# The output projection of four tiles in seven half-size products

## The chip, the cores and the metric

The kernel runs on one core of one Trainium2 chip. A core has a matrix engine (TensorE; PE in the profile, with PEld for its weight loads), VectorE (DVE), ScalarE (ACT), GpSimd (POOL) and SyncE (SP). Each takes its own instructions in order. PE writes its results into PSUM, eight banks of 128 partitions by 512 float32 columns; the other engines read operands from SBUF or PSUM, POOL from SBUF only. Semaphores hold an instruction back until the data that it needs are there. The metric is the device time of the program in microseconds, so lower is better.

## The reference

Four sequences of 768 tokens with eight heads of 64 pass through a block-wise linear attention with decay, and its output, 3072 rows of 512, goes through a gated feed-forward block:

```python
for b in range(nb):
    intra = np.einsum('bhic,bhjc->bhij', qb, kb) * Dmask[None]
    intra = np.einsum('bhij,bhjd->bhid', intra, vb)
    inter = np.einsum('bhid,bhde->bhie', qb * lam_pow[None], kv_state)
    out[:, :, sl] = intra + inter
    kv_state = lam_block[None, :, None, None] * kv_state + np.einsum('bhsd,bhse->bhde', kb_dec, vb)
...
g = x @ w_gate
silu = g * (1.0 / (1.0 + np.exp(-g)))
val = x @ w_val
return (silu * val @ w_out).astype(np.float32)
```

`w_gate` and `w_val` are 512 by 1536 and `w_out` is 1536 by 512. The change concerns only the last product, `h @ w_out`, with h = silu * val.

## The kernel before, in words

Tokens are worked off in six tiles (t = 0 to 5) of 512 tokens: four blocks of 128, which come from two attention groups of two blocks each. Group g belongs to tile g // 2.

For one tile the feed-forward part runs over twelve chunks of 128 columns of the hidden width (`ffn_fc`). A chunk is one step of the plan: four matmuls of 512 columns into a bank for the gate (L519), a Silu on ACT into a `sil` tile (L523), four matmuls into the next bank for the value (L534), and a product on DVE that reads that bank and writes one chunk of h in bfloat16 (L537). h is held in two tiles of six chunks each. The output projection `ffn_out` (L544 to L557) makes one block of 128 rows: twelve matmuls with a chunk of h as weights and 512 columns of `wo_sb` as the moving operand, all summed in one bank (L552), then a copy to an `osb` tile (L554) and a store to DRAM (L555). The very last block is made in a part of 384 columns and one of 128, so that its two copies and stores go through different engines.

PSUM banks are handed out in a ring of eight by `bank()`. Whoever takes a bank waits for the last reader of its former contents.

The order of work is written out by hand. `steps` holds the chunks of all tiles, and `plan` says what follows which step: `at(n, fn, ...)` appends a call. In tile t - 1, `attend(2t)` and `attend(2t + 1)` make the attention output that tile t reads. One call of `attend(g)` issues the inter-block matmuls of group g (L466), those for the state update of group g + 1 (L387), the scores of group g + 1 (L357), then the intra-block matmuls of g (L479). It needs v_s of group g + 1 (scaled by POOL, L243), its transposed q and k (`qkt`), and the running state (POOL, L426 to L437). `qkt` comes from `cast_scaled`: ACT casts k (L263), DVE scales q (L265), and SP issues a transposing DMA (L256). The loads of k, q and v go through SP (L107) into `raw` tiles, ten slots, and `v` tiles.

From tile 3 on, `cast_scaled` follows chunks 0 and 6, `attend` follows chunks 4 and 10, and the four output blocks of the tile before follow chunks 0, 3, 7 and 9. In tile 2 they follow chunks 1, 5, 7 and 9. The four blocks of tile 5 come at the end.

```python
for n, o in zip((1, 5, 7, 9) if t == 2 else (0, 3, 7, 9), outs):
    at(sn[n], ffn_out, *o)
outs = [(t, b) for b in range(4)]
```

Of the kernel before, what the change touches and what calls it, by code (L numbers as in the profile page):

```python
# [11 lines left out]
ALU = mybir.AluOpType  # L12
# [25 lines left out]
def _body(ctx, tc, nc, q, k, v, lam, moe_w_gate, moe_w_val, moe_w_out, out):  # L38
# [332 lines left out]
    def upd_mm(g, up=None):  # L371
        b, i = groups[g]
        v_s = st[("vs", g)]
        up = up or [bank() for _ in range(2)]
        started = set()
        for s in range(2):
            for hp in range(HP):
                for r in range(2):
                    if g >= NAT0 and i == NG // B - 1 and 2 * s + r == 3:
                        continue  # L380
                    for h2 in range(2):
                        ps = slice(r * M, r * M + M)
# [130 lines left out]
    def ffn_gate(t, fc, b0=0, b1=B):  # L513
        xt = st[("xt", t)]
        N = (b1 - b0) * BLK
        fs = slice(fc * 128, fc * 128 + 128)
        gp = bank()
        for mc in range(MC):
# [4 lines left out]
        nc.scalar.activation(sil[:, 0:N], gp[:, 0:N], AF.Silu)  # L523

    def ffn_val(t, fc, b0=0, b1=B):
        hn = ("h", t, fc // FH)
        if hn not in st:
            st[hn] = h_pool.tile([128, FH, B, BLK], BF16, name="h", tag="h")
        h_sb, xt, sil = st[hn], st[("xt", t)], st[("sil", t, fc, b0)]
        N = (b1 - b0) * BLK  # L530
        fs = slice(fc * 128, fc * 128 + 128)
        vp = bank()
        for mc in range(MC):
            nc.tensor.matmul(vp[:, 0:N], wv_sb[:, mc, fs],  # L534
                             xt[:, b0 // 2:b1 // 2, mc].rearrange("p g b n -> p g (b n)"),
                             start=(mc == 0), stop=(mc == MC - 1))
        nc.vector.tensor_tensor(out=h_sb[:, fc % FH, b0:b1].rearrange("p b n -> p (b n)"),  # L537
                                in0=sil[:, 0:N], in1=vp[:, 0:N], op=ALU.mult)
# [5 lines left out]
    def ffn_out(t, b, last=False):  # L544
# [3 lines left out]
            if last else ((0, DM, nc.scalar.copy, nc.scalar),)  # L548
        for c0, c1, fn, eng in halves:
            ps = bank()[:, 0:c1 - c0]  # L550
            for fc in range(FC):
                nc.tensor.matmul(ps, st[("h", t, fc // FH)][:, fc % FH, b], wo_sb[:, fc, c0:c1],  # L552
                                 start=(fc == 0), stop=(fc == FC - 1))
# [232 lines left out]
    at(s2, ffn_out, 0, 2)  # L786
    at(s2, ffn_out, 0, 3)

    outs = [(1, b) for b in range(4)]
    for t in range(2, NG // 2):  # L790
        sn = [step(t, fc, 2 if t == 2 and fc < NH else 0) for fc in range(FC)]
        if t == 2:
            at(sn[4], ahead, 6)
            at(sn[5], v_scale, 7, nc.vector)
# [7 lines left out]
        if t + 1 < NG // 2:  # L802
            at(sn[7 if t == 2 else 4], attend, 2 * t + 2)
            at(sn[10], attend, 2 * t + 3)
        for n, o in zip((1, 5, 7, 9) if t == 2 else (0, 3, 7, 9), outs):
            at(sn[n], ffn_out, *o)
        outs = [(t, b) for b in range(4)]

    for n, (t, fc, b0, b1) in enumerate(steps):
        if t >= 1 and t + 1 < NG // 2 and ("xt", t + 1) not in st:  # L810
            new_xt(t + 1)
        ffn_fc(t, fc, b0, b1)
        run_later(pace.get(n, 2 if len(later) > 1 else 1))
        for fn, a in plan.get(n, []):
            fn(*a)
            if fn in (attend, ahead):
                run_later(1)
    run_later(len(later))
    for t, b in outs:
        ffn_out(t, b, last=(b == 3))  # L820
# [1 line left out]
_INS = ['q', 'k', 'v', 'lam', 'moe_w_gate', 'moe_w_val', 'moe_w_out']  # L822
_OUTS = [((3072, 512), 'float32')]
# [25 lines left out]
```

## Time and profile before

| What | Value |
|---|---|
| median of three runs | 227.19 us |
| lowest and highest run | 226.88 and 227.25 us |
| span of the profiled execution, first to last instruction | 225.0 us (the only time given for that execution) |
| granted TensorE clock, mean | 1.000 |
| PE busy | 219.2 us, 97% of the span |
| DVE, ACT, POOL busy | 92.4, 106.5, 88.0 us |
| L519 and L534, gate and value matmuls | 77.2 and 77.1 us, 28% of the chain each |
| L552, output projection matmuls | 65.5 us, 28% of the chain |
| stores of 256 KB from `osb` | 23, median 2.9 us from issue to landing |

Matmuls are pipelined: one of 512 columns is recorded with 379 ns and one of 256 with 273, while they follow each other more closely than that. So the spacing is read from the chain, which shows runs of matmuls with their start and length, and not from the mean of one.

A row of a group gives line, engine, operation, output <- inputs, shapes and count, then busy time and mean of one, then the idle time of the engine just before these instructions and who ended it. In a time line each row is a start, a length, and what ran; the bracket at its end is idle time before it and its releaser. L12 is line 12 of the kernel.

### The profile page before, as it was taken

The numbers are of one execution on the slowest core, as the hardware profiler recorded it, in microseconds if no ns is written. First come the engines' busy times: TensorE is split into PE (matmuls) and PEld (weight loads), VectorE is DVE, ScalarE is ACT, GpSimd is POOL, SyncE is SP. The second block draws the span as 40 slices with busy tenths as digits, with TensorE's granted clock in tenths as the row PEclk, the third lists the DMA queues.
The fourth block names the chain that finished last, engine by engine and source line by source line (L and its number), as shares of the span: only waits on it lengthen the run. The fifth ranks groups of instructions, "written<-read, shape, count | busy, mean of one in ns | idle before, by whom it ended". The sixth has DMA issues, their size and how long they took to land.

```text
span 225.0 us, 6040 instructions
## 1 busy us (share of the span) xinstructions
PE 219.2 (97%) x2504; PEld 122.6 (54%) x2504; DVE 92.4 (41%) x159; ACT 106.5 (47%) x211; POOL 88.0 (39%) x131
## 2 busy tenths in 40 slices
PE   8989999999999999999999999999999999999994
PEld 4666455888886456454544544544544444444442
DVE  2664357576853712835345262253242123222200
ACT  5878586756462433564543543543533423322321
POOL 6674737837691120879553191191150000000000
PEclk9999999999999999999999999999999999999999
DMA  6999999999996999595788939806101101101122
GB/s 195 346 339 343 371 362 321 258 287 206 401 244 142 269 219 204 143 228 149 199 197 209 222 69 246 222 4 139 50 1 47 50 0 47 47 3 47 47 93 93
DMA packets 88028, 39.70 MB, mean 176 GB/s; under 512 B 57666, under 2 KB 83522, under 8 KB 88002
## 3 DMA queue, kind: packets, MB, share of 16 engines
q1 hardware_dynamic: 83490, 32.58, 57.1%
q10 hardware_dynamic: 4512, 6.75, 8.3%
q8 instruction: 19, 0.31, 0.6%
q14 instruction: 7, 0.06, 0.1%
HBM read 28.31 MB, written 6.29 MB: 154 GB/s over the span
## 4 chain that ended last, share of the span: by engine, by line
PE 95%; ACT 2%; DVE 1%; issue 1%; DVEq 0%
PE bank L519 28%; PE bank L534 28%; PE bank L552 28%; PE bank L479 2%; PE bank L466 2%; PE bank L387 2%; PE bank L131 1%; PE bank L331 1%; PE bank L357 1%; PE bank L294 1%; DVE ssb L338 1%; ACT qkt L296 1%; PE bank L166 0%; ACT qdec L188 0%; ACT L639 0%
## 5 line engine op out<-in xcount | busy, mean ns | idle before, releaser
L537 DVE TENSOR_TENSOR h<-sil,bank 128x512 bf16<-128x512 bf16 (+1 forms) x91 | 51.7, 575 | 101.5 <-PE bank L534 82.2
L519 PE MATMUL bank<-xt,wg_sb 128*128 128x512 bf16 (+1 forms) x364 | 77.2, 335 | 0.0
L534 PE MATMUL bank<-xt,wv_sb 128*128 128x512 bf16 (+1 forms) x364 | 77.1, 335 | 0.0
L523 ACT ACTIVATE sil<-bank 128x512 bf16<-128x512 f32 (+1 forms) x91 | 46.2, 512 | 42.9 <-PE bank L519 37.9
L552 PE MATMUL bank<-wo_sb,h 128*128 128x512 bf16 (+2 forms) x300 | 65.5, 371 | 0.0
L534 PEld LDWEIGHTS <-wv_sb 128*128 128x128 bf16 x364 | 35.4, 98 | 27.1 <-DVE wv_sb L689 0.5
L519 PEld LDWEIGHTS <-wg_sb 128*128 128x128 bf16 x364 | 34.4, 98 | 26.0 <-DVE xt L491 0.2
L552 PEld LDWEIGHTS <-h 128*128 128x128 bf16 x300 | 28.7, 98 | 32.6
L554 ACT COPY osb<-bank 128x512 f32<-128x512 f32 (+1 forms) x24 | 14.0, 582 | 56.2 <-PE bank L552 56.2
L243 POOL TENSOR_TENSOR v_s<-v,dec 128x1024 bf16<-128x1024 f32 (+1 forms) x14 | 21.7, 1556 | 20.7 <-DMA v<-in_v_dram 17.8
L426 POOL TENSOR_TENSOR kvf<-kvs,ups 128x256 f32<-128x256 f32 x8 | 5.8, 727 | 40.3 <-ACT ups L409 37.8
L338 DVE TENSOR_TENSOR ssb<-bank,causal 128x512 bf16<-128x512 f32 x24 | 15.4, 684 | 4.9 <-PE bank L331 4.9
L435 POOL CAST kvn<-kvf 64x256 bf16<-64x256 f32 x24 | 12.5, 520 | 1.5
L491 ACT CAST xt<-bank 128x512 bf16<-128x512 f32 x19 | 11.6, 658 | 3.0 <-PE bank L479 2.0
L426 POOL TENSOR_TENSOR kvf<-kvf,ups 128x256 f32<-128x256 f32 x16 | 11.6, 726 | 0.6
L409 ACT COPY ups<-bank 128x256 f32<-128x256 f32 (+1 forms) x24 | 9.5, 450 | 1.4 <-PE bank L387 0.9
L263 ACT CAST qk<-kraw 128x1024 bf16<-128x1024 f32 x9 | 9.4, 1043 | 0.8 <-DMA kraw<-in_k_dram 0.8
L265 DVE TENSOR_TENSOR qk<-qraw,qdn 128x1024 bf16<-128x1024 f32 x6 | 8.0, 1328 | 2.1 <-DMA qraw<-in_q_dram 2.1
L362 DVE TENSOR_TENSOR ssb<-bank,causaln 128x512 bf16<-128x512 f32 x12 | 8.3, 688 | 1.2 <-PE bank L357 1.1
L479 PE MATMUL bank<-ssb,v_s 64*64 64x128 bf16 (+1 forms) x384 | 6.7, 207 | 0.3 <-ACT guard L450 0.3
L387 PE MATMUL bank<-v_s,qk 64*64 64x64 bf16 x352 | 5.8, 195 | 0.5 <-issue 0.5
L479 PEld LDWEIGHTS <-v_s 64*64 64x64 bf16 x384 | 5.5, 105 | 1.3 <-issue 0.7
(68 smaller groups left out, 124.9 us busy)
## 6 DMA issues: line engine op xcount, KB each, us to landing
out_dram<-osb ACTq DMA_DIRECT2D x23, 256.0 KB, 2.9
v<-in_v_dram SPq DMA_DIRECT2D x18, 256.0 KB, 4.6
woraw<-in_moe_w_out_dram SPq DMA_DIRECT2D x6, 512.0 KB, 7.7
kraw<-in_k_dram SPq DMA_DIRECT2D x24, 128.0 KB, 3.6
qraw<-in_q_dram SPq DMA_DIRECT2D x24, 128.0 KB, 3.6
wraw<-in_moe_w_gate_dram SPq DMA_DIRECT2D x5, 512.0 KB, 6.9
wraw<-in_moe_w_val_dram SPq DMA_DIRECT2D x5, 512.0 KB, 6.9
kraw<-in_k_dram SPq DMA_DIRECT2D x4, 512.0 KB, 6.6
```

Source lines behind the costliest of these rows:

```text
L243: eng.tensor_tensor(out=st[("vs", g)][:, h0:h1], in0=st[("v", g)][:, h0:h1].rearrange("p h (s d) -> p h s d", s=2), in1=vfac(g, h0, h1), o ...
L338: nc.vector.tensor_tensor(out=ssb[:, h2, 2 * c:2 * c + 2].rearrange("p a s n -> p a (s n)"), in0=sp[(c, h2)].rearrange("p (a x) -> p a x", ...
L426: nc.gpsimd.tensor_tensor(out=o, in0=f, in1=u, op=ALU.add)
L435: nc.gpsimd.tensor_copy(out=o[64 - h2 * 64:128 - h2 * 64], in_=f[h2 * 64:h2 * 64 + 64])
L479: nc.tensor.matmul(op[r][h2 * 64:h2 * 64 + 64, cols(g, hp, s)], v_s[ps, 2 * hp + h2, s], ssb[ps, h2, hp * 2 + s] if g >= NAT0 else ssb[ps, ...
L491: fns[r](out=xt[:, g % 2, :, r].rearrange("p h (m s) -> p h s m", s=2) if g < NAT0 else xt[:, g % 2, :, :, r * M:r * M + M], in_=op[r].rea ...
L519: nc.tensor.matmul(gp[:, 0:N], wg_sb[:, mc, fs], xt[:, b0 // 2:b1 // 2, mc].rearrange("p g b n -> p g (b n)"), start=(mc == 0), stop=(mc = ...
L523: nc.scalar.activation(sil[:, 0:N], gp[:, 0:N], AF.Silu)
L534: nc.tensor.matmul(vp[:, 0:N], wv_sb[:, mc, fs], xt[:, b0 // 2:b1 // 2, mc].rearrange("p g b n -> p g (b n)"), start=(mc == 0), stop=(mc = ...
L537: nc.vector.tensor_tensor(out=h_sb[:, fc % FH, b0:b1].rearrange("p b n -> p (b n)"), in0=sil[:, 0:N], in1=vp[:, 0:N], op=ALU.mult)
L552: nc.tensor.matmul(ps, st[("h", t, fc // FH)][:, fc % FH, b], wo_sb[:, fc, c0:c1], start=(fc == 0), stop=(fc == FC - 1))
L554: fn(out=osb[:, c0:c1], in_=ps)
```

## The change

The projection of tiles 2 to 5 goes from `ffn_out` to `out_units`. A unit is one group: its two blocks of 128 rows are the two row blocks of a 2 by 2 scheme. The inner dimension is split into chunks 0 to 5 and 6 to 11 of h, and the output columns into two halves of 256. Strassen's scheme in Winograd's form makes the four quarter results from seven products of a quarter's size, each six matmuls of 256 columns, where eight products would be made directly.

The products need sums of operands. On W: three tiles `wt` and one that replaces the upper right quarter of `wo_sb`, each made in three pieces (`wo_combo`). On h: for a pair of chunks (two from each half), four instructions (`h_combo`); three results go to new tiles `hs`, and one replaces the odd blocks of the first half of h. All are DVE instructions on bfloat16 in SBUF. `wt` and `hs` take slots of the `raw` pool.

A unit uses three banks. The first product goes into bank `a`; ACT copies it into bank `b`, where later products add to it without clearing it. [...] The second product goes into bank `e`, and ACT copies it to an SBUF tile `es`. DVE twice adds `b` and `es`: once into bank `e`, once into the output tile. ACT copies the other three quarters, and each unit makes two stores of 256 KB.

The order changes too. In tiles 3 to 5 the chunks run in the order 0, 1, 6, 7, 2, 3, 8, 9, 4, 5, 10, 11, so that a pair is complete after every four steps. The two units of a tile follow steps 5 and 8 of the next tile. The operand sums follow single steps, one to three at a time; the last pair of a tile is summed after steps 0 to 3 of the next. In the tables of steps below `sn[n]` is the n-th step of tile t. The last tile's two units come at the end, their first two products one unit after the other, then the other five of each.

```diff
+    def take(n, seeded, cols):
+        was = [primed.get((ring[0] + i) % 8, 0) >= cols for i in range(n)]
+        got = [bank() for _ in range(n)]
+        j = was.index(True)
+        got[seeded], got[j] = got[j], got[seeded]
+        return got
...
+    def wo_combo(n, j):
+        fs, fz = slice(2 * j, 2 * j + 2), slice(FH + 2 * j, FH + 2 * j + 2)
+        b11, b12 = wo_sb[:, fs, 0:HD], wo_sb[:, fs, HD:DM]
+        b21, b22 = wo_sb[:, fz, 0:HD], wo_sb[:, fz, HD:DM]
+        if n < 3 and n not in wt:
+            wt[n] = raw_pool.tile([128, FH, HD], BF16, name="wt", tag="raw")
+        w = [wt[i][:, fs] if i in wt else None for i in range(3)]
+        o, i0, i1 = ((w[0], b12, b11), (w[1], b22, w[0]), (w[2], b21, w[1]), (b12, b22, b12))[n]
+        nc.vector.tensor_tensor(out=o, in0=i0, in1=i1, op=ALU.subtract)
+
+    def h_combo(t, j, n, eng=nc.vector):
+        fs = slice(2 * j, 2 * j + 2)
+        ha, hb = st[("h", t, 0)], st[("h", t, 1)]
+        a11, a21 = ha[:, fs, 0:B:2], ha[:, fs, 1:B:2]
+        a12, a22 = hb[:, fs, 0:B:2], hb[:, fs, 1:B:2]
...
+        s = [st[("hs", t, i)][:, fs] for i in range(3)]
+        o, i0, i1, op = ((s[0], a21, a22, ALU.add), (s[1], s[0], a11, ALU.subtract),
+                         (a21, a11, a21, ALU.subtract), (s[2], a12, s[1], ALU.subtract))[n]
+        eng.tensor_tensor(out=o, in0=i0, in1=i1, op=op)
...
+    def out_units(t, gs):
...
+        for g in gs:
+            bs = take(3, 1, HD)
+            u[g] = ([x[:, 0:HD] for x in bs],
+                    [osb_pool.tile([128, DM], FP32, name="osb", tag="osb") for _ in range(2)],
+                    kv_pool.tile([128, HP, D], FP32, name="es", tag="kvf", bufs=4).rearrange("p h d -> p (h d)"))
+
+        def product(g, k, lhs, rhs, start):
+            o = u[g][0][k]
+            for fc in range(FH):
+                nc.tensor.matmul(o, lhs(fc), rhs(fc), start=(start and fc == 0), stop=(fc == FH - 1),
+                                 skip_group_check=True)
...
+        for g in gs:
+            (a, b, e), (o0, o1), es = u[g]
+            product(g, 0, lambda f: ha[:, f, 2 * g], lambda f: wo_sb[:, f, 0:HD], True)
+            nc.scalar.copy(out=b, in_=a)
+            product(g, 2, lambda f: ha[:, f, 2 * g + 1], lambda f: wo_sb[:, f, HD:DM], True)
+            nc.scalar.copy(out=es, in_=e)
+        for g in gs:
+            (a, b, e), (o0, o1), es = u[g]
+            product(g, 1, lambda f: s2[:, f, g], lambda f: wt[1][:, f], False)
+            nc.vector.tensor_tensor(out=e, in0=b, in1=es, op=ALU.add)
+            product(g, 0, lambda f: hb[:, f, 2 * g], lambda f: wo_sb[:, FH + f, 0:HD], False)
+            nc.scalar.copy(out=o0[:, 0:HD], in_=a)
+            product(g, 1, lambda f: s1[:, f, g], lambda f: wt[0][:, f], False)
+            nc.vector.tensor_tensor(out=o1[:, HD:DM], in0=b, in1=es, op=ALU.add)
+            product(g, 2, lambda f: hb[:, f, 2 * g + 1], lambda f: wt[2][:, f], False)
+            nc.scalar.copy(out=o1[:, 0:HD], in_=e)
+            store(g, 1)
+            product(g, 1, lambda f: s4[:, f, g], lambda f: wo_sb[:, FH + f, HD:DM], False)
+            nc.scalar.copy(out=o0[:, HD:DM], in_=b)
+            store(g, 0)
...
-    outs = [(1, b) for b in range(4)]
+    outs = [(ffn_out, 1, b) for b in range(4)]
...
-        sn = [step(t, fc, 2 if t == 2 and fc < NH else 0) for fc in range(FC)]
+        order = [c for j in range(FC // 4) for c in (2 * j, 2 * j + 1, FH + 2 * j, FH + 2 * j + 1)]
+        sn = [step(t, fc, 2 if t == 2 and fc < NH else 0) for fc in (range(FC) if t == 2 else order)]
...
-        for n, o in zip((1, 5, 7, 9) if t == 2 else (0, 3, 7, 9), outs):
-            at(sn[n], ffn_out, *o)
-        outs = [(t, b) for b in range(4)]
+        for n, o in zip((1, 5, 7, 9) if t == 2 else (5, 8), outs):
+            at(sn[n], *o)
+        if t == 2:
+            for n in range(9):
+                at(sn[n + 2], wo_combo, n // 3, n % 3)
+            for n in range(4):
+                at(sn[8 + n], h_combo, t, 0, n)
+        else:
+            for n in range(4):
+                at(sn[4 + n], h_combo, t, 0, n)
+                at(sn[8 + n], h_combo, t, 1, n)
+                if t == 3:
+                    at(sn[n // 2], h_combo, t - 1, 1, n)
+                    at(sn[2 + n // 2], h_combo, t - 1, 2, n)
+                else:
+                    at(sn[n], h_combo, t - 1, 2, n)
+                if t == 3 and n < 3:
+                    at(sn[n], wo_combo, 3, n)
+        outs = [(out_units, t, (g,)) for g in range(2)]
...
-    for t, b in outs:
-        ffn_out(t, b, last=(b == 3))
+    for n in range(4):
+        h_combo(NG // 2 - 1, 2, n)
+    out_units(NG // 2 - 1, (0, 1))
```

More of the change, by code (lines that the diff above doesn't have):

```diff
@@ L78, in _body, with covered @@
     ring = [0]
+    primed = {}
     def bank():
         b = banks[ring[0] % 8]
+        primed[ring[0] % 8] = 0
         ring[0] += 1
         return b
+    def covered(cols, n=1):
+        for i in range(n):
+            primed[(ring[0] - 1 - i) % 8] = cols
     def gsrc(t, g, h0):
@@ L373, in upd_mm @@
         v_s = st[("vs", g)]
-        up = up or [bank() for _ in range(2)]
+        if up is None:
+            up = [bank() for _ in range(2)]
+            covered(HP * D, 2)
         started = set()
@@ L496, in core_a @@
         st[("op", g)] = [bank() for _ in range(2)]
+        covered(2 * HP * D, 2)
         inter(g, True)
@@ L517, in ffn_gate @@
         gp = bank()
+        covered(N)
         for mc in range(MC):
@@ L532, in ffn_val @@
         vp = bank()
+        covered(N)
         for mc in range(MC):
@@ L550, in ffn_out @@
             ps = bank()[:, 0:c1 - c0]
+            covered(c1 - c0)
             for fc in range(FC):
@@ L557, in ffn_out @@
                           in_=osb[:, c0:c1])
+    def take(n, seeded, cols):
[4 more added lines that the diff above has]
+        return got
+    HD = DM // 2
+    wt = {}
+    def wo_combo(n, j):
[7 more added lines that the diff above has]
+        nc.vector.tensor_tensor(out=o, in0=i0, in1=i1, op=ALU.subtract)
@@ new lines, in h_combo @@
+    def h_combo(t, j, n, eng=nc.vector):
[3 more added lines that the diff above has]
+        a12, a22 = hb[:, fs, 0:B:2], hb[:, fs, 1:B:2]
+        for i in range(3):
+            if ("hs", t, i) not in st:
+                st[("hs", t, i)] = raw_pool.tile([128, FH, B // 2, BLK], BF16, name="hs", tag="raw")
+        s = [st[("hs", t, i)][:, fs] for i in range(3)]
+        o, i0, i1, op = ((s[0], a21, a22, ALU.add), (s[1], s[0], a11, ALU.subtract),
+                         (a21, a11, a21, ALU.subtract), (s[2], a12, s[1], ALU.subtract))[n]
+        eng.tensor_tensor(out=o, in0=i0, in1=i1, op=op)
@@ new lines, in out_row, with store @@
+    def out_row(t, b):
+        g = groups[2 * t + b // 2]
+        return g[0] * S + (g[1] * 2 + b % 2) * BLK
+    def out_units(t, gs):
+        ha, hb = st[("h", t, 0)], st[("h", t, 1)]
+        s1, s2, s4 = [st[("hs", t, i)] for i in range(3)]
+        u = {}
+        for g in gs:
[8 more added lines that the diff above has]
+                                 skip_group_check=True)
+        def store(g, r):
+            nc.scalar.dma_start(out=bass.AP(tensor=out.tensor, offset=out.offset + out_row(t, 2 * g + r) * DM,
+                                            ap=[[DM, 128], [1, DM]]), in_=u[g][1][r])
+        for g in gs:
[18 more added lines that the diff above has]
+            store(g, 0)
@@ L787, in _body @@
     at(s2, ffn_out, 0, 3)
-    outs = [(1, b) for b in range(4)]
+    outs = [(ffn_out, 1, b) for b in range(4)]
+    late_steps = {}
     for t in range(2, NG // 2):
-        sn = [step(t, fc, 2 if t == 2 and fc < NH else 0) for fc in range(FC)]
+        order = [c for j in range(FC // 4) for c in (2 * j, 2 * j + 1, FH + 2 * j, FH + 2 * j + 1)]
+        sn = [step(t, fc, 2 if t == 2 and fc < NH else 0) for fc in (range(FC) if t == 2 else order)]
         if t == 2:
@@ L813, in _body @@
         run_later(pace.get(n, 2 if len(later) > 1 else 1))
-        for fn, a in plan.get(n, []):
+        for fn, *a in [(f, *x) for f, x in plan.get(n, [])]:
             fn(*a)
```

## The prediction

> **What bounds the kernel now.** I read the page first (who is busy, the chain), then the chain in order of time, then the groups with their shapes kept apart, then the time lines of DVE, POOL and SP around tiles 2 and 3.
>
> ```profile
> PE 219.2 (97%) x2504; PEld 122.6 (54%) x2504; DVE 92.4 (41%) x159; ACT 106.5 (47%) x211; POOL 88.0 (39%) x131
> ...
> PE 95%; ACT 2%; DVE 1%; issue 1%; DVEq 0%
> ```
>
> PE is busy 97% of the span and makes 95% of the chain: time goes only if PE's list shortens, and any wait that PE newly meets is paid in full.
>
> ```profile
> 69.07 0.44 PE bank L534 x4
> 69.51 2.59 PE bank L552 x12
> ...
> 114.80 2.59 PE bank L552 x12
> ...
> 126.89 0.38 PE bank L466 x32
> ...
> 211.49 10.40 PE bank L552 x60
> ```
>
> These are pieces of the chain (start, length, matmuls). Four 256-column matmuls take 0.44 us; eleven such pieces, 64.70 to 69.51, make 4.81/44 = 0.1093 us each. Twelve of 512 columns take 2.59, 0.216 each. The 2.59 at 114.80 is the output block at tile 3's chunk 0; 126.89 is the attention of group 8 (chunk 4). The last tile's projection, 10.40, ends at 221.89, the span 3.1 later.
>
> ```profile
> L537 DVE TENSOR_TENSOR h<-sil,bank 128x512 bf16<-128x512 bf16 x53 | 36.4, 688 | 83.2 <-PE bank L534 77.1 <-ACT sil L523 4.5 <-PE bank L331 1.5
> ...
> L537 DVE TENSOR_TENSOR h<-sil,bank 128x256 bf16<-128x256 bf16 x38 | 15.3, 418 | 18.3 <-ACT sil L523 13.1 <-PE bank L534 5.2
> ...
> L300 DVE TENSOR_TENSOR qkt<-bank,qdec 128x256 bf16<-128x256 bf16 x12 | 2.8, 284 | 0.2 <-PE bank L294 0.2
> ```
>
> The price of one two-operand DVE instruction. With a float32 bank, 256 more columns cost 270 ns (418 to 688), so 148 ns are fixed. L300, all of 16 bits (its bank holds bfloat16), takes 284 for 256 columns, 136 above the fixed part: half the rate.
>
> ```profile
> 114.91 0.69 DVE L537 TENSOR_TENSOR h<-sil,bank 128x512 bf16<-128x512 bf16 x1
> 117.67 1.23 DVE L265 TENSOR_TENSOR qk<-qraw,qdn 128x1024 bf16<-128x1024 f32 x1 [2.07 <-DMA qraw<-in_q_dram]
> 119.22 0.69 DVE L537 TENSOR_TENSOR h<-sil,bank 128x512 bf16<-128x512 bf16 x1 [0.33 <-PE bank L534]
> ```
>
> ```profile
> 119.53 1.91 POOL L243 TENSOR_TENSOR v_s<-v,dec 128x1024 bf16<-128x1024 f32 x1 [3.71 <-DMA v<-in_v_dram]
> ...
> 131.97 1.90 POOL L435 CAST kvn<-kvf 64x256 bf16<-64x256 f32 x2
> ```
>
> ```profile
> 119.04 1.91 SPq L256 DMA_TRANSPOSE qkt<-qk  x1
> ```
>
> At tile 3's chunk 0 DVE stands 2.07 us for group 9's q, then scales it (L265), and only then may multiply chunk 1. That costs nothing now, for the output block keeps PE busy from 114.80 to 117.39. The pair of POOL casts took 1.90 us, against 0.85 for the pair at 129.10: L265 ran from 132.40 to 133.62 and the second cast ended just after it.
>
> **The change part by part.**
>
> *Products.* Before, a unit (two blocks) is 24 matmuls of 0.216 = 5.18 us. After, it is 7 x 6 = 42 of 0.1093 = 4.59. Eight units save 8 x 0.59 = 4.7 us. Their weight loads (98 ns each in the rows) go beside the stream: the 0.1093 was taken where every matmul loads its own.
>
> [...]
>
> *Handovers inside a unit.* Consumers start 0.04 (ACT) or 0.11 us (DVE) after a piece ends (136.00 to 136.04; 131.68 to 131.79), and PE resumes 0.2 after them: 0.04 (178.09 to 178.13) and the 0.16 by which a 256-column matmul's 273 ns outlast its spacing. A product lasts 0.656. The seed copy takes the 0.381 of L409's 256-column row: 0.04 + 0.38 + 0.2 = 0.62, hidden by the next product. Each of the two DVE additions over `b` takes the 0.418 of L537: 0.11 + 0.42 + 0.2 = 0.73, hidden but for 0.075. So 0.15 a unit, 1.2 in all. No row has an engine write a float32 sum into a bank: from 0 (284 ns, the cheapest row) to 0.7 a unit (688 ns). I take 418, the same columns with one bank operand. If ACT's Silu or DVE's h product stood in front, up to 0.6 would come on top; at chunks 5 and 8 both are done by then.
>
> *Operand sums.* 12 on W and 12 a tile on h, of 512 bfloat16 columns: 60 DVE instructions. By L300's rate 148 + 272 = 0.42 us, 0.40 from start to start (neighbours overlap by up to 0.08). Bounds: 0.28 (L300 as it is) and 0.69 (L537). L300 is nearest, its operands being all of 16 bits. That is 24 us on an engine 59% idle: free except in two places.
>
> *First place: tile 3, chunks 0 to 4.* Tile 2 runs on PE as before, so chunk 0 still ends at 114.80. The output blocks of chunks 0 and 3 are gone (units now follow chunks 5 and 8), so PE reaches chunk 4's end at 114.80 + 4 x 1.727 = 121.71 and group 9's scores, after 0.38 + 0.25 of attention matmuls, at 122.34. DVE is held by q until 117.67 as now; SP's loads are not moved. Behind the scaling come 3 sums, h of chunk 1, 3 sums, h of chunk 2, 3 sums, h of chunk 3: 118.80 + 9 x 0.40 + 2 x 0.61 + 0.69 = 124.3. The scores take the two banks of chunk 3 (eight banks in a ring: chunk 3, chunk 4, two, two, then these), so they wait for that h: 124.5 instead of 122.34, 2.2 us. In this stretch POOL's v_s of group 9 (1.91, ready at 119.53) meets the sums. It can start at the latest beside h of chunk 1, about 120.0, and keeps the next sums from 120.6 to 121.9; DVE lost 0.38 of 0.52 us of overlap at 90.82 (1.60 instead of 1.22), about 0.7 of it, so 0.9 more: **3.1 us**; without the clash 2.2, and the time 228.4. The floor is SP's transpose, issued at 119.04, landing 3.9 later, 122.9: 0.8. The ceiling is with sums at 0.61 apart: 5.0.
>
> That POOL's cast waited out all of L265 is the row for this. [...] No run here shows it for 16-bit sums.
>
> *Other attention steps.* In tile 2, 9 W sums and 4 h sums can hold POOL back by 0.42 each; before group 6's attention (98.02) POOL ends its state at 96.88 and three sums lie in between, 1.26: 0.1. Group 10 comes after 10.4 us of PE instead of 15.6; its chain (scaling, transpose 3.7 to 5.0 to land) just fits: 0.2, at most 0.8. SP's q of group 11 may wait for a `raw` slot until chunk 8's unit; v queues behind it; both land some 2 us before use: 0.
>
> *Second place: the end.* After chunk 11, DVE has h (0.11 to 0.80), one sum left of pair 1, then three until a11-a21 of pair 2: four at about 0.42 from 0.72, so 2.4, and PE goes on at 2.6. PE has product `a` and four of six matmuls of `e` before it, 1.09. So 1.5 us (1.0 to 2.5). Before, eleven matmuls of the first block covered it.
>
> Two units at once want four `osb` out of three: the fourth waits for the first store to land. A late store takes 2.0, which just reaches: 0.2 (0 to 0.6).
>
> The last store is 256 KB behind a 0.38 copy: 0.07 + 0.38 + 0.02 + 2.0 + 1.1 (from the 64 KB's landing, 222.29 + 1.6, to 225.0) = 3.6 against 3.1: 0.5.
>
> **Sum.** -4.7 + 1.2 + 3.1 + 0.1 + 0.2 + 1.5 + 0.2 + 0.5 = +2.1 us. The only time shown for an execution with a profile is its span, 225.0; the runs have 227.19, 2.2 more for what lies around it, which I keep. 225.0 + 2.1 = 227.1; **229.3 us.**
>
> **Rivals.**
> 1. *DVE keeps up* (ends on the other side). If the sums come every 0.24 us or less, h of chunk 3 is ready when the transpose lands, and the first place costs 0.8: 227.0. If the seams are then hidden too (-1.2), 225.8. For: L300 at 284 has fewer columns only. Against: it would need 512 columns at less than L300 takes for 256. That point, h of chunk 3 by 122.9, decides the sign.
> 2. *Sums at full price* (0.69, 0.61 apart). First place 5.0, end 2.5: 229.3 + 1.9 + 1.0 = 232.2. For: their blocks are strided. Against: L300's `qdec` is strided too.
> 3. *Seams cost more*: copies and additions queue behind Silu, h or sums, 0.3 a unit: +2.4, 231.7. For: DVE's order is fixed. Against: the units stand ahead of their chunk's sums.
> 4. *No shorter products*: weight loads (98 ns) that show, or the seeding, make 42 matmuls no cheaper than 24. From 0.123 us a matmul the saving is gone: at least 4.7 more, 234.0. The 0.44 rows speak against it. [...]
>
> **How the numbers follow.** My case 0.52; its own range, 227.4 to 230.8, takes the first place at 2.2 to 3.5, the seams at 0 to 2.2 and the end at 1.0 to 2.0. Rival 1 has 0.24, rival 2 0.13, rival 3 0.10, rival 4 0.01. The whole range, 226.2 to 232.2, leaves out rival 1 with hidden seams (0.14), rival 4 and a little above rival 2. A measurement cannot tell 0.2%, 0.45 us, from no change: 226.7 to 227.6. Rival 1 gives faster 0.14 (seams hidden) and same 0.10; the low tail of mine gives 0.03 and 0.05. So faster 0.17, same 0.15, slower 0.68.
>
> **What would show it.** Products every 0.109 us. PE idle before L357 at group 9's scores, its releaser the h product; around there POOL's v_s or DVE sums longer than their like elsewhere. Sums near 420 ns. PE idle about 1.5 us in the last tile's second product, released by a DVE subtraction. Inside units gaps under 0.1. I am wrong if PE runs through group 8's attention unbroken, if the sums take 0.3 or 0.7, or if units show gaps of 0.3.

## The result, and the profile after

The changed kernel takes 230.06 us (median of 4 runs, 229.38 to 230.35), the kernel before 227.22 in the same comparison. The ratio is 1.0124, with a 95% interval from 1.0104 to 1.0144: slower, as forecast, by 2.8 us where 2.1 had been worked out. The ratios below leave out executions over 1.5% above the fastest of their kernel.

The profiled execution took 229.38 us, with a span of 227.7 at a clock of 0.999: 2.7 us over the span before. First the page and the groups with their shapes apart:

```profile
PE 215.6 (95%) x2636; PEld 135.6 (60%) x2636; DVE 126.1 (55%) x234; ACT 112.0 (49%) x235; POOL 88.4 (39%) x131
...
L610 DVE TENSOR_TENSOR hs<-h 128x512 bf16<-128x512 bf16 x12 | 8.8, 732 | 0.0
L610 DVE TENSOR_TENSOR hs<-hs,h 128x512 bf16<-128x512 bf16 x12 | 5.0, 418 | 0.1
L647 DVE TENSOR_TENSOR bank<-bank,es 128x256 f32<-128x256 f32 x8 | 3.5, 431 | 9.0 <-PE bank L631 9.0
L641 ACT COPY bank<-bank 128x256 f32<-128x256 f32 x8 | 2.9, 357 | 6.8 <-PE bank L631 6.8
```

PE's list is shorter by 3.6 us of recorded time, and yet the span is longer: PE's share fell from 97% to 95%. An undisturbed operand sum takes 418 ns, an addition into a bank 431, the copy from bank to bank 357 (`take` only chooses which of the unit's three banks receives it, and emits no instruction). The mean of 732 in the first L610 row says that some sums took far longer. The chain has the units as pieces (start, length, matmuls):

```profile
128.45 4.71 PE bank L631 x42
138.34 1.99 PE bank L631 x18
141.76 2.15 PE bank L631 x18
162.08 4.71 PE bank L631 x42
```

A unit of seven products, 42 matmuls, takes 4.71 us where eight took 5.18. One unit, from 138.34 to 143.91, takes 5.57: it is broken off in the middle. PE's time line shows all its longer waits from 110 us on, there, at the attention of group 8 and at the end:

```profile
122.61 0.21 PE L475 MATMUL bank<-qkt,kv 64*64 64x64 bf16 x1
...
124.07 0.35 PE L396 MATMUL bank<-v_s,qk 64*64 64x64 bf16 x18 [0.98 <-DVE h L549]
...
125.80 0.44 PE L364 MATMUL bank<-qkt 64*64 64x64 bf16 x30 [1.28 <-DVE h L549]
...
126.44 1.04 PE L530 MATMUL bank<-xt,wg_sb 128*128 128x512 bf16 x4
...
141.76 0.82 PE L631 MATMUL bank<-wt,hs 128*128 128x256 bf16 x6 [0.80 <-DVE bank L647]
...
215.51 1.70 PE L631 MATMUL bank<-wo_sb,h 128*128 128x256 bf16 x14 [1.22 <-DVE h L610]
```

The two waits at the attention are the first place of the prediction, which named only the second, before the scores (L364). The first comes one h product earlier, before the state update (L396), and takes its share out of the same delay. The wait at the end (L631 at 215.51) was forecast too; the one at 141.76 was not. From the first L475 to the next gate matmul (L530) the attention takes 3.83 us (122.61 to 126.44). Behind its two waits stand the time lines of DVE and POOL:

```profile
118.46 1.22 DVE L272 TENSOR_TENSOR qk<-qraw,qdn 128x1024 bf16<-128x1024 f32 x1 [1.67 <-DMA qraw<-in_q_dram]
119.61 0.42 DVE L610 TENSOR_TENSOR hs<-h 128x512 bf16<-128x512 bf16 x1
119.94 0.42 DVE L595 TENSOR_TENSOR wo_sb<-wo_sb 128x512 bf16<-128x512 bf16 x1
120.28 0.42 DVE L610 TENSOR_TENSOR hs<-hs,h 128x512 bf16<-128x512 bf16 x1
120.61 0.68 DVE L549 TENSOR_TENSOR h<-sil,bank 128x512 bf16<-128x512 bf16 x1
121.21 1.54 DVE L595 TENSOR_TENSOR wo_sb<-wo_sb 128x512 bf16<-128x512 bf16 x1
122.67 0.41 DVE L610 TENSOR_TENSOR h<-h 128x512 bf16<-128x512 bf16 x1
...
123.34 0.67 DVE L549 TENSOR_TENSOR h<-sil,bank 128x512 bf16<-128x512 bf16 x1
...
125.06 0.68 DVE L549 TENSOR_TENSOR h<-sil,bank 128x512 bf16<-128x512 bf16 x1
```

```profile
120.27 2.19 POOL L250 TENSOR_TENSOR v_s<-v,dec 128x1024 bf16<-128x1024 f32 x1 [3.37 <-DMA v<-in_v_dram]
```

DVE scales group 9's q late, then works off sums and h products without a pause. The sum that meets POOL's v_s takes 1.54 us instead of 0.42 and ends 0.29 after v_s does. So h of the chunks ahead of the attention is late, the state update and the scores find no free bank until the h products of 123.34 and 125.06 are done, and PE stands.

### The profile page after: what moved, and what is told of

It reads as the page before. It is cut to its first block, busy times and chain, and to the rows that moved or that the text cites. A ratio compares the mean times of both kernels' runs of the same rounds, so it can differ in the third digit from the quotient of the medians.

```text
span 227.7 us, 6416 instructions
## 1 busy us (share of the span) xinstructions
PE 215.6 (95%) x2636; PEld 135.6 (60%) x2636; DVE 126.1 (55%) x234; ACT 112.0 (49%) x235; POOL 88.4 (39%) x131
## 4 chain that ended last, share of the span: by engine, by line
PE 55%; DMA 11%; SPq 10%; POOL 10%; issue 7%; DVE 4%; ACT 1%; ACTq 0%; POOLq 0%; DVEq 0%
PE bank L530 18%; PE bank L546 17%; PE bank L631 16%; DMA qraw<-in_q_dram 6%; SPq L114 5%; SPq L107 3%; POOL kvf L435 3%; DMA wraw<-in_moe_w_val_dram 3%; DMA v<-in_v_dram 2%; SPq L225 2%; POOL kvn L444 2%; POOL v_s L250 2%; PE bank L488 1%; DVE h L549 1%; DVE hs L610 1%
## 5 line engine op out<-in xcount | busy, mean ns | idle before, releaser
L530 PE MATMUL bank<-xt,wg_sb 128*128 128x512 bf16 (+1 forms) x364 | 77.2, 335 | 0.0
L530 PEld LDWEIGHTS <-wg_sb 128*128 128x128 bf16 x364 | 34.4, 98 | 24.7
L250 POOL TENSOR_TENSOR v_s<-v,dec 128x1024 bf16<-128x1024 f32 (+1 forms) x14 | 22.8, 1635 | 23.1 <-DMA v<-in_v_dram 18.9
L565 PE MATMUL bank<-wo_sb,h 128*128 128x512 bf16 x96 | 21.9, 379 | 0.0
L631 PEld LDWEIGHTS <-h 128*128 128x128 bf16 x192 | 18.7, 98 | 5.1 <-DVE h L610 1.5
L631 PE MATMUL bank<-wo_sb,h 128*128 128x256 bf16 x144 | 18.3, 273 | 1.2 <-DVE h L610 1.2
L631 PEld LDWEIGHTS <-hs 128*128 128x128 bf16 x144 | 13.9, 97 | 3.7 <-issue 1.0
L565 PEld LDWEIGHTS <-h 128*128 128x128 bf16 x96 | 9.2, 98 | 10.4
L631 PE MATMUL bank<-wt,hs 128*128 128x256 bf16 x96 | 13.0, 271 | 0.8 <-DVE bank L647 0.8
L567 ACT COPY osb<-bank 128x512 f32<-128x512 f32 x8 | 4.7, 586 | 16.6 <-PE bank L565 16.6
L444 POOL CAST kvn<-kvf 64x256 bf16<-64x256 f32 x24 | 11.2, 465 | 1.5
```

The lines of the kernel that those rows point to most:

```text
L250: eng.tensor_tensor(out=st[("vs", g)][:, h0:h1], in0=st[("v", g)][:, h0:h1].rearrange("p h (s d) -> p h s d", s=2), in1=vfac(g, h0, h1), o ...
L444: nc.gpsimd.tensor_copy(out=o[64 - h2 * 64:128 - h2 * 64], in_=f[h2 * 64:h2 * 64 + 64])
L530: nc.tensor.matmul(gp[:, 0:N], wg_sb[:, mc, fs], xt[:, b0 // 2:b1 // 2, mc].rearrange("p g b n -> p g (b n)"), start=(mc == 0), stop=(mc = ...
L631: nc.tensor.matmul(o, lhs(fc), rhs(fc), start=(start and fc == 0), stop=(fc == FH - 1), skip_group_check=True)
```

## The experiments

Each kernel below was run 6 or 12 times, in three groups: e1 to e4 together, c1 to c4 together, c5 to c7 together, each group on one chip with 23 to 35 runs of the kernel before (medians 227.27, 227.10 and 226.97 us).

**e1: a slot for the third sum tile of tile 3.** DVE's time line of the changed kernel around the third wait:

```profile
140.35 0.42 DVE L610 TENSOR_TENSOR hs<-h,hs 128x512 bf16<-128x512 bf16 x1 [2.60 <-PE bank L631]
140.69 0.68 DVE L549 TENSOR_TENSOR h<-sil,bank 128x512 bf16<-128x512 bf16 x1
141.29 0.42 DVE L647 TENSOR_TENSOR bank<-bank,es 128x256 f32<-128x256 f32 x1
```

DVE stood 2.60 us before the first write into `hs` number three of tile 3, released by a product of tile 2's last unit. `raw` has ten slots; `wt` holds three for good, tile 2's `hs` three, tile 3's first two `hs` two, and loads the rest, so this one had to wait for a slot that only this unit gives back. The unit's own addition (L647) was queued behind it. The edit takes that one tile from the pool of h:

```diff
-                st[("hs", t, i)] = raw_pool.tile([128, FH, B // 2, BLK], BF16, name="hs", tag="raw")
+                pool, tag = (h_pool, "h") if (t, i) == (3, 2) else (raw_pool, "raw")
+                st[("hs", t, i)] = pool.tile([128, FH, B // 2, BLK], BF16, name="hs", tag=tag)
```

> Only the third operand-sum tile of tile 3 gets a slot of its own (in the pool of h, which has one free); all work is done. Seen in the changed kernel: in the unit after chunk 8 of tile 3 PE stands 0.80 us for the DVE addition, because one sum ahead of it on DVE started 2.6 us late, at 140.35, after a product of the same unit. Theory: that sum had to wait for a slot of the raw pool, which a tile of tile 2 gave back only in this unit; so the unit takes 4.7 us instead of 5.6, and the time falls by 0.8, to 229.3. Rival: it was held by POOL's read of SBUF, or by PE for another reason; then the unit keeps its 5.6 us and the time stays at 230.1.

Measured: 228.44 us, ratio 1.0045 (1.0014 to 1.0077). In its profile the sum runs at once and the unit is unbroken:

```profile
136.34 0.41 DVE L611 TENSOR_TENSOR hs<-h,hs 128x512 bf16<-128x512 bf16 x1
...
139.09 0.43 DVE L648 TENSOR_TENSOR bank<-bank,es 128x256 f32<-128x256 f32 x1 [1.28 <-PE bank L632]
```

The slot is the cause of that wait. The time fell by more than its 0.8; c1 below shows where the rest comes from.

**e2: no sums ahead of group 8's attention.** The sums of tile 2's later two pairs of chunks and the last one on W are left out; tile 2's products use the first pair's sums in their place, so as many matmuls run as before.

```diff
-                if t == 3:
-                    at(sn[n // 2], h_combo, t - 1, 1, n)
-                    at(sn[2 + n // 2], h_combo, t - 1, 2, n)
-                else:
+                if t > 3:
                     at(sn[n], h_combo, t - 1, 2, n)
-                if t == 3 and n < 3:
-                    at(sn[n], wo_combo, 3, n)
```

> Leaves out the operand sums between chunks 0 and 3 of tile 3 (eight on h, three on W): the units of tile 2 take the sums of the first pair of chunks three times, and the upper right quarter of W stays as it is. Output is not the reference's; PE does all its products. Theory (the sums behind the late q delay h of chunk 3, and with it the bank that group 9's scores need): PE's wait in the attention of group 8 falls from 2.6 us to the floor set by the transpose of group 9, about 0.8; the time to about 228.3. Rival (it is the order alone: with the output blocks gone from chunks 0 and 3, PE comes before q, v and the transpose are there, whatever the sums do): the wait stays at 2.2 or more and the time at 229.7 to 230.1.

Measured: 226.38 us, ratio 0.9965 (0.9936 to 0.9993). The waits for h are gone, which speaks for the theory, though the time lies below what either side had set. In the profiled execution another wait had taken their place:

```profile
123.56 0.35 PE L396 MATMUL bank<-v_s,qk 64*64 64x64 bf16 x19 [1.91 <-POOL v_s L250]
```

There v had come late from DRAM: POOL stood 6.0 us for it, against 3.4 in the changed kernel. So what is late next, once DVE keeps up, can be POOL's v_s and not only SP's transpose, which the prediction had named.

**e3: no v_s beside the sums.** Group 9's v_s is left out, and its matmuls read that of group 8.

```diff
-                if g > 7:
+                if g == 9:
+                    at(sn[1 + j], lambda: st.update({("vs", 9): st[("vs", 8)]}))
+                elif g > 7:
                     at(sn[1 + j], v_scale, g, nc.gpsimd)
```

> Leaves out one POOL instruction, the scaling of v of group 9: group 9 uses the scaled v of group 8. Output is not the reference's. Theory (POOL and DVE shut each other out while both read SBUF operands): the sum that took 1.54 us beside it takes 0.42, h of chunk 3 is done 1.1 us earlier, the wait before group 9's scores falls from 2.6 to about 1.5, the time to 229.0. Rival (the long sum has another cause, such as the dependence on the projection that still reads W): it stays at 1.5 us and the time at 230.1.

Measured: 227.82 us, ratio 1.0019 (0.9994 to 1.0044). With POOL quiet the same sums come every 0.34 us, none over 0.42:

```profile
119.07 0.42 DVE L610 TENSOR_TENSOR hs<-h 128x512 bf16<-128x512 bf16 x1
119.41 0.42 DVE L595 TENSOR_TENSOR wo_sb<-wo_sb 128x512 bf16<-128x512 bf16 x1
119.74 0.41 DVE L610 TENSOR_TENSOR hs<-hs,h 128x512 bf16<-128x512 bf16 x1
120.08 0.68 DVE L549 TENSOR_TENSOR h<-sil,bank 128x512 bf16<-128x512 bf16 x1
120.67 0.41 DVE L595 TENSOR_TENSOR wo_sb<-wo_sb 128x512 bf16<-128x512 bf16 x1
...
124.34 0.95 DVE L610 TENSOR_TENSOR hs<-h,hs 128x512 bf16<-128x512 bf16 x1
```

The L595 at 120.67 is the one that took 1.54. Of the two waits at the attention one is left, 0.74 us before L364. From the first L475 to the next gate matmul (L530) the stage takes 2.2 us (122.56 to 124.78) instead of 3.8 (122.61 to 126.44). Of these 1.6, 1.1 are the sum that is no longer stretched and 0.5 that q, and so DVE's work, came 0.5 us earlier in this execution.

**e4: the last sums of tile 5 made early.** The difference a11 - a21 of tile 5 goes to a tile of its own instead of over a21, so it need not wait for the other sums, and that of the last pair follows step 10:

```diff
-                         (a21, a11, a21, ALU.subtract), (s[2], a12, s[1], ALU.subtract))[n]
+                         (s[3] if last else a21, a11, a21, ALU.subtract), (s[2], a12, s[1], ALU.subtract))[n]
...
+        if t == NG // 2 - 1:
+            at(sn[10], h_combo, t, 2, 2)
...
-    for n in range(4):
+    for n in (0, 1, 3):
         h_combo(NG // 2 - 1, 2, n)
```

> In tile 5 the difference of the first-half row blocks goes to a tile of its own instead of over its operand; its last pair, which needs only chunks 4 and 5, is summed after step 10 instead of after chunk 11. All work is done. Theory (PE's wait of 1.4 us in the second product of the end is the chain h, three sums on DVE): the wait goes, since the next sums are wanted only after four more products, 2.6 us; time falls by 1.4, to 228.7. Rival (another wait takes its place: the third output buffer, or the sum wanted by the third product): less than half of it comes back, 229.4 or more.

Measured: 228.20 us, ratio 1.0032 (0.9999 to 1.0066). The chain now ends in one unbroken piece of 78 matmuls where it had 68 behind the wait:

```profile
212.14 8.75 PE bank L633 x78
```

All four came out lower than expected of them. Either the runs recorded for the changed kernel were not typical, or something was missing from the account. So the kernel itself was run again beside the next ones.

**c1: the changed kernel again.**

> The changed kernel itself, nothing edited, beside the variants below. If the four runs recorded for it stand for it, 230.1 us and a ratio to the kernel before of 1.0124. If three of those four owed some of their time to the lower mean granted clock that they showed (0.991 against 0.999 in the profiled one, which took 229.38), then 229.2 to 229.5 and a ratio near 1.009.

Measured: 229.95 us (229.01 to 232.20), ratio 1.0127 (1.0079 to 1.0176): the recorded result holds. But its six executions are of two kinds: 229.01 and 229.05 us at a mean granted clock of 0.998 and 0.999, and 229.74 to 232.20 at 0.990 to 0.993. The profiled one is of the second kind, and shows where the clock went. Columns: stretch, its length, busy time of PE, PEld, DVE, ACT and POOL with instructions, PEclk, DMA share, GB/s.

```profile
123.00:124.50 1.50, 0.59 (x35) 0.37 (x35) 1.50 (x4) 0.16 (x1) 0.04 (x1) 1.00 0.82 184
124.50:126.00 1.50, 0.44 (x24) 0.33 (x24) 1.47 (x5) 0.85 (x2) 0.18 (x1) 1.00 0.85 192
126.00:127.50 1.50, 1.13 (x63) 1.00 (x63) 1.50 (x4) 0.10 (x2) 1.38 (x3) 0.66 0.88 200
127.50:129.00 1.50, 1.50 (x5) 0.47 (x4) 1.38 (x3) 0.98 (x2) 1.35 (x3) 0.50 0.90 207
129.00:130.50 1.50, 1.50 (x7) 0.70 (x6) 0.00 (x0) 0.60 (x1) 1.38 (x4) 0.70 0.94 208
130.50:132.00 1.50, 1.50 (x16) 1.33 (x15) 1.29 (x2) 0.49 (x2) 0.23 (x1) 1.00 0.77 172
```

From 123 to 126 PE is busy for 1.03 of 3 us: the waits of group 8's attention. Then the clock is 0.66, 0.50 and 0.70 for 4.5 us, which costs about 1.5 x (0.34 + 0.50 + 0.30) = 1.7 us, and is back at 1. So the waits may be paid for twice. This was a new theory, and c2 and c5 were to test it.

A second reason why e1 to e4 came out low lies ahead of the change. Tile 1's first attention matmul, before any edited step, began anywhere from 61.89 to 63.92 us in the thirteen traces: at 63.38 and 63.92 in the two of the changed kernel, at 62.34, 63.32 and 61.95 in those of e1, e3 and e4. Counted from that matmul to the end of the span, and all four at a clock of 0.999 or more, the changed kernel takes 164.3 us and e1, e3 and e4 take 163.2, 162.9 and 163.3. That is 1.2, 1.4 and 1.1 less, where 0.8, 1.1 and 1.4 had been expected. Whether the late start of the changed kernel's two traces is chance, no run shows.

**c2: tile 2 undone.** Tile 2 goes back to its four output blocks of `ffn_out`, behind steps 0, 3, 7 and 9 of tile 3 as in the kernel before; its sums are gone. Tiles 3 to 5 keep seven products.

```diff
-        for n, o in zip((1, 5, 7, 9) if t == 2 else (5, 8), outs):
+        for n, o in zip((1, 5, 7, 9) if t == 2 else (0, 3, 7, 9) if t == 3 else (5, 8), outs):
...
-            for n in range(4):
-                at(sn[8 + n], h_combo, t, 0, n)
...
-                if t == 3:
-                    at(sn[n // 2], h_combo, t - 1, 1, n)
-                    at(sn[2 + n // 2], h_combo, t - 1, 2, n)
-                else:
+                if t > 3:
                     at(sn[n], h_combo, t - 1, 2, n)
                 if t == 3 and n < 3:
-                    at(sn[n], wo_combo, 3, n)
-        outs = [(out_units, t, (g,)) for g in range(2)]
+                    at(sn[9 + n], wo_combo, 3, n)
+        outs = [(ffn_out, t, b) for b in range(4)] if t == 2 else [(out_units, t, (g,)) for g in range(2)]
```

> Tile 2 goes back to eight full products per pair; tiles 3, 4 and 5 keep seven. Theory (the first place is DVE's sums for tile 2 in front of the attention of group 8, and tile 2's sums also take the raw slots that tile 3 lacks later): against the changed kernel's profiled 229.4 us, the two units of tile 2 give up 2 x (0.59 - 0.15) = 0.9 us, the waits there give back 2.6 and the wait in tile 3's first unit 0.8, so 226.9 us, a ratio of 0.998 to 1.000; no PE wait at L364 or L396 on h or v_s above 0.3 us around the attention of group 8. Rival (the wait there comes from the late q and v_s alone, whatever DVE does): the waits stay at 2.6 us, and the time is 229.5 us.

Measured: 226.38 us, ratio 0.9962 (0.9935 to 0.9990), and no execution of twelve under a clock of 0.997. The attention of group 8 runs through, from the first L475 at 126.53 to the gate at 127.77:

```profile
126.81 0.36 PE L396 MATMUL bank<-v_s,qk 64*64 64x64 bf16 x20
...
127.04 0.48 PE L364 MATMUL bank<-qkt 64*64 64x64 bf16 x30
127.35 0.49 PE L488 MATMUL bank<-ssb,v_s 64*64 64x64 bf16 x32
127.77 1.04 PE L530 MATMUL bank<-xt,wg_sb 128*128 128x512 bf16 x4
```

1.24 us against 3.83 in the changed kernel, so its waits there cost 2.6. This alone does not put the rival out: with the two output blocks back, PE comes to the attention at 126.53 instead of 122.61, and late q and v would be covered too. c4 decides that. Two units fewer in seven products, and the kernel is 3.6 us faster than the control; at a full clock it is 2.7 (226.38 against 229.03), where 2.5 had been worked out.

**c3: tile 2 undone, and the end mended.** c2 with the edit of e4, and the last store in two halves of 128 KB, the first on SP's queue as soon as its half is copied:

```diff
+        def half(g, c, eng):
+            eng.dma_start(out=bass.AP(tensor=out.tensor, offset=out.offset + out_row(t, 2 * g) * DM + c,
+                                      ap=[[DM, 128], [1, HD]]), in_=u[g][1][0][:, c:c + HD])
...
             nc.scalar.copy(out=o0[:, 0:HD], in_=a)
+            if s3 is not None and g == 1:
+                half(g, 0, nc.sync)
```

> The kernel of the line above, and at the end the last sums of tile 5 made early enough (the wait of 1.4 us before product e goes) and the last store in two halves of 128 KB on two queues (some 0.2 to 0.3 us of the 0.5 added there). Theory: 1.6 us below the one above, 225.3 us, a ratio of 0.991. Rival (the sum moved into step 10 delays the last units' operands instead): no better than the one above, 226.9 us.

Measured: 224.48 us, ratio 0.9881 (0.9846 to 0.9916). This one beats both kernels. From the start of the last product to the end of the span it takes 4.11 us (217.99 to 222.1), in the changed kernel 4.46 (223.24 to 227.7). The account closes: six units at 4.71 instead of 5.18 save 2.8 us, the last store costs some 0.2, so 226.98 - 2.6 = 224.4, with 226.98 the kernel before at a full clock in this group.

**c4: all four tiles, tile 2's sums behind the attention of group 8.** The edits of e1 and of c3's end, and:

```diff
-        for n, o in zip((1, 5, 7, 9) if t == 2 else (5, 8), outs):
+        for n, o in zip((1, 5, 7, 9) if t == 2 else (7, 9) if t == 3 else (5, 8), outs):
...
+                    at(sn[4 + n // 2], h_combo, t - 1, 1, n)
+                    at(sn[5 + n // 2], h_combo, t - 1, 2, n)
+                    if n < 3:
+                        at(sn[4 + n // 2], wo_combo, 3, n)
+                    at(sn[8 + n // 2], h_combo, t, 0, n)
+                    at(sn[10 + n // 2], h_combo, t, 1, n)
```

> All four tiles keep seven products. Tile 2's later sums are moved behind the attention of group 8, its units behind steps 7 and 9 of tile 3, the third sum tile of tile 3 takes a slot of h, and the end is as in the line above. Theory: of the changed kernel's profiled 229.4 us, 1.4 + 0.25 go at the end, 0.8 in tile 3's first unit and 1.8 to 2.6 at the attention of group 8, so 224.6 to 225.4 us, a ratio of 0.989 to 0.992. Rival (the sums only move their delay: h of the chunks behind attention 8 comes late instead, by the 0.42 us of each of 11 sums less the idle time of DVE there): a new wait of 1 to 2 us on h in steps 4 to 7 of tile 3, and 226 to 227 us.

Measured: 228.88 us over all twelve, ratio 0.9971 (0.9926 to 1.0016), which rests on six of them. The attention is unbroken, although PE is there at 121.97, as early as in the changed kernel, and q comes as late (DVE scales it at 117.52). So it was the sums, and c2's rival is out. But PE stands before the first unit of tile 2, and the clock is 0.5 from 133.5 to 139.5:

```profile
133.48 0.61 PE L634 MATMUL bank<-wo_sb,h 128*128 128x256 bf16 x2 [3.60 <-DVE h L612]
```

c4's own rival was right, and by more than it said: the delay only moved. DVE is busy from 123 to 134 us, and a sum again meets a v_s, that of the next group (DVE, then POOL):

```profile
131.30 2.12 DVE L612 TENSOR_TENSOR h<-h 128x512 bf16<-128x512 bf16 x1
```

```profile
131.13 2.01 POOL L250 TENSOR_TENSOR v_s<-v,dec 128x1024 bf16<-128x1024 f32 x1 [2.78 <-DMA v<-in_v_dram]
```

**c5 and c6: a wait made on purpose.** c2, with one product of SiLU and value, in the step ahead of group 8's attention, repeated in place, six times in c5 and three times in c6:

```diff
-        nc.vector.tensor_tensor(out=h_sb[:, fc % FH, b0:b1].rearrange("p b n -> p (b n)"),
-                                in0=sil[:, 0:N], in1=vp[:, 0:N], op=ALU.mult)
+        for _ in range(6 if (t, fc) == (3, 2) else 1):
+            nc.vector.tensor_tensor(out=h_sb[:, fc % FH, b0:b1].rearrange("p b n -> p (b n)"),
+                                    in0=sil[:, 0:N], in1=vp[:, 0:N], op=ALU.mult)
```

> The kernel with tile 2 undone (226.4 us, mean clock 0.997 or more in all its 12 runs), and in step 4 of tile 3, right ahead of the attention of group 8, the product of SiLU and value taken six times over instead of once into the same place: 5 x 0.60 = 3.0 us more of DVE, for which PE must wait before L364 (2.8 to 3.2 us in one piece). Theory (a PE wait of this length sometimes lowers the granted clock for the few us behind it, at a price of its own of some 1.6 us): runs of two kinds, 229.3 us at a mean clock of 0.997 or more and 230.5 to 231.5 at 0.993 or less, with at least a third of the runs of the second kind. Rival (the lower clock of the changed kernel has nothing to do with its waits): all runs at 0.997 or more, 229.3 us.

Measured: 230.03 us, ratio 1.0100 (1.0064 to 1.0136). Twelve executions, two kinds with nothing between: five at a clock of 0.997 to 0.999 with 227.78 to 228.42 us, seven at 0.990 to 0.992 with 230.00 to 231.23. The wait fell a little later than expected and is shorter, since the bank came to be missed only at the next value matmuls. Behind it the clock goes down:

```profile
132.04 1.61 PE L546 MATMUL bank<-xt,wv_sb 128*128 128x512 bf16 x4 [2.25 <-DVE h L550]
```

```profile
130.00:132.00 2.00, 0.00 (x0) 0.00 (x0) 1.93 (x4) 0.69 (x2) 1.80 (x5) 1.00 0.77 173
132.00:134.00 2.00, 1.96 (x6) 0.77 (x6) 1.16 (x3) 0.00 (x0) 1.80 (x4) 0.58 0.01 1
134.00:136.00 2.00, 2.00 (x7) 0.72 (x6) 1.91 (x3) 0.61 (x2) 1.62 (x1) 0.56 0.00 0
```

The wait itself costs some 1.8 us (226.38 to the 228.18 of the first kind), the lower clock 2.4 more in the second kind, of which the last two stretches show 2 x (0.42 + 0.44) = 1.7. c5 adds to c2 only five DVE products and the wait that they make, and c2 had no execution under 0.997 in twelve. c6, with two of these products and no wait, had none either, on the same chip as c5. So it is the wait that brings the lower clock; by what means, and why only in seven of twelve, no run shows.

> The same with three products instead of one: 2 x 0.60 = 1.2 us more of DVE and a PE wait of 1.0 to 1.5 us. Theory: the wait alone, 227.5 us, with none or few runs at a mean clock under 0.995. Rival (any wait there lowers the clock): as many runs at 0.993 as with the long wait, median 228.5 us or more.

Measured: 226.68 us, ratio 0.9996 (0.9972 to 1.0020), no execution under 0.997. But PE did not wait: 1.2 us more of DVE stayed covered, and the profile has no PE wait over 0.3 us there. So it says nothing on short waits; it only shows that 1.2 us more of work on DVE lowered no clock while PE stayed busy.

**c7: tile 2's units later still.** c4 with `(10, 11) if t == 3`.

> The kernel with all four tiles in seven products, the sums of tile 2 behind the attention of group 8 and the mended end, but its units of tile 2 behind steps 10 and 11 of tile 3 instead of 7 and 9. In the run before this one PE stood 3.6 us before the first of these units for the sums (h L612), with DVE busy without a break from 123 to 134 us and the clock at 0.5 for the 6 us after. Theory (the sums fit if the units come after them): the 3.6 us go to under 1 us and the clock stays up, so 224 to 225 us, level with the kernel with tile 2 undone and the mended end (224.5). Rival (DVE has no room for tile 2's sums anywhere in tile 3, or the slots held longer make loads late): a new wait of 1 to 3 us in steps 8 to 11 of tile 3 or at tile 4's first chunks, 226 us or more.

Measured: 229.35 us over all twelve, ratio 0.9967 (0.9920 to 1.0014), which rests on four of them. The one wait of 3.60 became several:

```profile
124.46 0.35 PE L396 MATMUL bank<-v_s,qk 64*64 64x64 bf16 x19 [1.59 <-POOL v_s L250]
136.59 0.19 PE L475 MATMUL bank<-qkt,kvn 64*64 64x64 bf16 x1 [0.53 <-DVE h L549]
138.58 0.44 PE L364 MATMUL bank<-qkt 64*64 64x64 bf16 x30 [0.95 <-DVE h L549]
140.56 2.54 PE L634 MATMUL bank<-wo_sb,h 128*128 128x256 bf16 x12 [1.26 <-DVE h L549]
```

The first of them is not the sums: v came late, as in e2 (POOL stood 5.64 us for it). A fifth, of 0.80 us, came at 150.26 behind DVE's mask (L369). DVE is busy from 125 to 141 us almost without a break. The rival holds: in these two arrangements there was no room in tile 3 for tile 2's sums beside its own, the mask, the scaling of q and the h products. At a clock of 0.997 or more c7 takes 226.3 us, c4 226.9, c3 224.5.

## Why the prediction came out as it did

The forecast, 229.3 us, stands 0.8 under the median, inside its own range, and on the right side. By its terms:

- *Products, -4.7.* Right. The chain's pieces hold 42 matmuls in 4.71 us with the seams; c3 confirms it over six units. Rival 4 is out: 42 loads for 42 matmuls, and still 0.112 us each.
- *Handovers, +1.2.* 4.71 - 4.59 = 0.12 a unit, 1.0 in all. The additions took 0.431 and 0.424 against 0.418, the seed copy 0.357 against 0.381. In one unit DVE's h product did stand in front of an addition, which the prediction had excluded: next point.
- *The slots, 0.* Wrong. The prediction asked only whether SP's load of q would wait for a `raw` slot. The third `hs` tile of tile 3 waited for one, in front of an addition of the unit that was to free it: 5.57 - 4.71 = 0.86 us, gone in e1. Rival 3's mechanism, in a single unit.
- *Operand sums, 0.42 each.* Right; but start to start they are 0.34 apart, not 0.40.
- *First place, +3.1.* The mechanism right, the size 2.6 (3.83 - 1.24). Nine sums at 0.06 less make the 0.5 of difference. The clash with POOL cost 1.1 where 0.9 was set, in the place named; smaller differences, such as PE's restart 0.06 us after h where 0.2 was set, offset that. For 16-bit operands the clash is now in the traces: 1.54 beside v_s, 0.41 without it (e3).
- *The end, +1.5.* 1.39: behind the ten matmuls from 213.03, at 0.109 each, the next could have followed at 214.12, and it ran at 215.51. e4 takes the wait away.
- *Small ones.* Tile 2's attention 0.1: nothing before group 6's, 0.1 around group 7's (from there to group 8's 11.94 us, where before it was 17.00 with two blocks of 2.59). Group 10's attention 0.2 and the third `osb` buffer 0.2: neither wait is there. The last store 0.5: 0.53.

Sum of the measured terms: -4.7 + 1.0 + 0.86 + 2.6 + 0.1 + 1.39 + 0.53 = +1.8, where the spans differ by 2.7. In this execution the part that no edit touches was 0.84 us late (tile 1's attention began at 63.38 instead of 62.54), which leaves 1.9 for the change. All but 0.1 of that is in the sum. At a full clock the control took 229.03, in two executions only, and the kernel before 226.98: +2.05, and 2.1 had been forecast. One part of that agreement is luck: the missed 0.86 was offset by the 0.2 of the handovers, 0.5 of the first place, 0.1 of the end and 0.4 of waits that did not come.

What the prediction lacked altogether is the clock. It counted each wait once. In seven of the ten executions of the changed kernel, counting the control, the mean clock was 0.993 or less; the one of these with a trace has the lower clock right behind the waits at group 8's attention and nowhere else. Those seven took 229.7 to 232.2 us, the other three 229.0 to 229.4. The median is of the former kind, and so lies above the forecast.

Rival 1 needed sums every 0.24 us; they come every 0.34, and e3 shows that even without the clash a stage of 2.2 us, 1.0 too long, was left. Rival 2 (0.69) is out. The choice of 0.42 us a sum from the 16-bit row was the step that decided between these two and mine.

## What to carry to other kernels

A scheme that takes multiplications from the bounding engine gives its additions to another one: ask not for that engine's share over the span (DVE 55%) but for its room in the one stage where its products gate the next matmuls; undoing a quarter of this change there turned 1.2% slower into 0.4% faster, and mending the end into 1.2% faster. Follow each new tile to the slot it takes and ask who gives that slot back, and whether that one is queued behind it. And a wait of TensorE can cost more than its length: c5's cost some 1.8 us, and in seven of twelve executions 2.4 more through the lower clock behind it.

## What the runs showed that was not expected

**A wait can lower the clock behind it.** Executions with a mean granted clock under 0.995, over all runs with a clock on record, with the PE waits at group 8's attention (in c4, c5 and c7 at the places shown above) in the one trace of each kernel:

| kernel | PE waits there, us | executions under 0.995 | median of the others, us | median of these, us |
|---|---|---|---|---|
| before | none over 0.3 | 12 of 87 | 226.9 to 227.0 | 228.4 to 229.1 |
| c2, c3, c6 | none over 0.3 | 0 of 30 | 226.4, 224.5, 226.7 | |
| e3 | 0.74 | 1 of 12 | 227.8 | 231.0 |
| e2 | 1.91 (v late in this execution) | 2 of 12 | 226.2 | 228.9 |
| e1 | 0.70 and 1.28 | 5 of 12 | 227.6 | 229.7 |
| changed, c1 | 0.98 to 1.06 and 1.28 | 7 of 10 | 229.0 (c1) | 230.8 (c1) |
| e4 | 1.13 and 1.28 | 7 of 12 | 227.1 | 228.8 |
| c5 | 2.25 | 7 of 12 | 228.2 | 230.6 |
| c4, c7 | 3.60; up to 1.59 | 14 of 24 | 226.9, 226.3 | 229.7, 229.8 |

With about 2.0 us or more of PE waiting within some 4 us in the trace (e1, the changed kernel with c1, e4, c5, c4 and c7), 40 of 70 executions have it, their medians 1.6 to 3.5 us longer; with 0.74 (e3) it is 1 of 12. The five traces that have the lower clock (c1, c4, c5, c7 and e2) show it right behind such waits and nowhere else; in c7's it stayed at 1.00 behind the single 1.59 and fell to 0.50 behind the three later ones. In c5's trace 2.25 us in one piece was enough (0.58 and 0.56 behind it), and in e2's 1.91 (0.70 from 126 to 130 us). Why the kernel before has it in 12 of 87 executions, with no such wait in its one profile, was not tried.

**A sum caught by a v_s lasted until just after that v_s ended.** A 512-column sum of 0.42 us took 1.54, 2.12 and 2.13 beside a v_s of 2.19, 2.01 and 2.08 (at 121.21 in the changed kernel, 131.30 in c4, 108.03 in the changed kernel). In the twelve traces with seven products, 34 sums were caught by a v_s, and each ended 0.27 to 0.29 us after it.
